# A linear-attention and feed-forward block on one core: later second x tile, block map on GpSimd, key and value products in two parts

## The chip, the core and the metric

The kernel runs on one core of a Trainium2 chip. Its engines run beside each other, each in its own program order: TensorE (PE, matrix products, with weight loads shown as PEld), VectorE (DVE), ScalarE (ACT), GpSimd (POOL) and SyncE (SP, which issues most of the transfers). They wait for each other through semaphores. The metric is the device time of one execution in microseconds (us).

## The reference

The input x has 2048 rows of 640 values, in bf16. The part that matters:

```python
def _A_ref(x, wqkv, w_phi, wo):          # H = 32 heads of Dh = 20
    q, k, v = split(x @ wqkv)
    pq = jnp.einsum("bhsd,hdf->bhsf", q, w_phi)
    pk = jnp.einsum("bhsd,hdf->bhsf", k, w_phi)
    phi_q = concat([softmax(pq), softmax(-pq)])
    phi_k = concat([softmax(pk), softmax(-pk)])
    kv  = jnp.einsum("bhsf,bhsd->bhfd", phi_k, v)
    z   = jnp.einsum("bhsf->bhf", phi_k)
    num = jnp.einsum("bhqf,bhfd->bhqd", phi_q, kv)
    den = jnp.einsum("bhqf,bhf->bhq", phi_q, z)[..., None] + 1e-6
    return (num / den).reshape(B, S, D) @ wo
def _B_ref(x, w1, w2):
    return silu(x @ w1) @ w2             # 640 -> 1728 -> 640
h  = x + _A_ref(layernorm(x), A_wqkv, A_w_phi, A_wo)
h2 = h + _B_ref(layernorm(h), B_w1, B_w2)
```

## The kernel before

The rows are cut into 16 tiles of 128 tokens (index t); the 640 features are five chunks of 128 (index c). The kernel is not written as loops over tiles. Each step is a small function `op_...`, and a long string `ORDER` lists the calls one by one, for all engines together: `kp.0@2` calls `op_kp(0)` with its PSUM result from bank 2 on, `xn.2.a` calls `op_xn(2, "a")`. The order of the calls is the order of the instructions on each engine; nothing reorders them. A letter at the end picks the engine: `v` DVE, `a` ACT, `p` POOL, `s` the SP queue for a transfer. PSUM has eight banks; a call that writes banks waits until what stood in them has been read.

The start, in words. `lx` loads tiles of x, `lk` chunks of the key weights, `lv` of the value weights, `lp` the small feature weights w_phi. `wm` is a product of constants into a bank that nobody reads; 14 of these stand at the head of PE's order and between its first steps. The feature weights are folded into the key weights: `wt` transposes a chunk of the key weights on PE, `wc` copies it out of PSUM (wTk), `mk` makes a mask with block-diagonal ones on POOL, `ph` multiplies w_phi with it into a block map `phb`, `fk` multiplies wTk with phb on PE, and `fc` casts the result into the folded weights Wfk, on ACT. `gk`, `gc` do the same for the query weights, whose transposed chunks come by a transposing transfer, `lq`.

For each tile: `st` takes the statistics (two halves and their sum, DVE), `rs` the reciprocal root with a power on POOL, `xn` the normalised tile; `xt` and `xc` transpose it through PE and PSUM, or `xd` by a transposing transfer on the SP queue. `kp` is the key projection with the folded weights, `vp` the value projection: ten products each, over five chunks and two halves of the output. `ke` takes the exponentials on ACT (plus and minus), `kr` their sums on DVE, `kn` divides (POOL, DVE or both by share: `p` all on POOL, `q` 48 of 64 groups, `b` 32, `d` 16, `v` none). `vc` copies the values out. `cc` sums keys times values into PSUM bank 7 over all tiles; `kc` and `km` turn the sum into the block matrix KVBD.

Then `qp`, `qs`, `qr`, `qt` are the query products in four parts (two, three, two and three products), `qe` their exponentials (EqT). `dp` multiplies EqT of one tile with KVBD into four PSUM banks, and `dw`, `dr`, `do` on DVE and POOL make num / den of it; `td` transposes that through SP. `op` multiplies with wo, `oa` adds to x, `sq`, `sr`, `hn`, `hd` are the second normalisation and transpose, `up`, `ua` the first feed-forward product and its silu, `yp`, `yh` the second, `yo`, `yz` add and store.

The order ends with the two parts of tile 13. Transfers are followed by eight semaphores in turn, so that the ninth transfer waits until the first has landed.

Of the kernel before, what the change touches and what calls it, by code (L numbers as in the profile page):

```python
# [30 lines left out]
lx.12.16.s vp.1@6 st.10 xt.2@5 vp.0@0 xc.2.a xn.9.a vc.0.a vp.2@2 st.11 lo.2.5.s xn.3.v xt.3@4 xc.3.a  # L31
rs.10.12 xn.8.a vc.2.a vc.1.a kp.2@0 ke.2 st.4 xd.9 st.5 kp.3@4 lo.0.2.s ke.3 rs.4.6 vp.3@2 xn.11.v vp.9@6
vc.9.a xn.4.a kp.9@0 ke.9 vc.3.a st.12 st.13 st.6 rs.12.14 xd.8 kr.1 kn.1.p kp.8@4 ke.8 mc.1 xn.13.a xn.12.a
xd.11 vp.11@6 vp.8@0 vc.8.a xn.5.v kr.0 kp.11@2 lq.2.s ke.11 st.7 rs.6.8 xn.6.a st.14 st.15 rs.14.16 xd.4
kr.9 vp.4@4 vc.4.a xd.5 vp.5@0 kn.0.p vc.11.a kr.2 vc.5.a kn.9.p kp.5@2 kr.11 kn.11.p gk.2@4 xn.10.a gc.2.a
xd.12 vp.12@6 vc.12.v kr.3 kn.3.p kp.4@0 xn.15.a ke.4 kp.12@4 cc.9 cc.1 kr.4 kn.4.p cc.0 xn.14.v cc.11 ke.5
kr.5 kn.2.d xd.13 ke.12 kr.12 lq.4.s xd.6 kp.6@0 lq.0.s ke.6 vp.13@2 vc.13.a kp.13@4 ke.13 vp.6@0 xd.15
xd.10 gk.4@2 vp.10@4 vc.6.a lq.3.s gk.3@0 gc.4.a gc.3.a vc.10.a kn.5.q kp.10@2 kn.12.p kr.6 xn.7.a l1.3.s
kn.6.q lq.1.s gk.1@0 gc.1.a kr.13 kn.13.p cc.4 cc.5 l1.0.s ke.10 kr.10 cc.2 cc.3 cc.12 xd.14 xd.7 kr.8
kn.8.p kn.10.d vp.15@4 vc.15.a kp.15@0 ke.15 kp.14@2 gk.0@4 gc.0.a vp.7@0 ke.14 kr.14 kn.14.p qp.0.1@4  # L40
# [10 lines left out]
dw.7.p dr.7 up.0.3@4 ua.0.3 do.6.0.p dp.8@0 dw.8.p dr.8 hn.2.a up.0.1@6 ua.0.1 td.6 do.8.0.p op.5@4 oa.5
dp.12@0 dw.12.p dr.12 yp.1.0@6 do.7.1.p do.7.0.p sq.5 td.7 hd.3 op.4@4 oa.4 sr.5 hn.5.v hd.5 do.9.1.p sq.4
td.9 sr.4 hn.4.a dp.10@0 dw.10.p yp.1.1 yp.0.1@4 yh.0.0 hd.2 hd.4 yo.1 dp.11@0 dw.11.p dr.11 do.8.1.p
do.11.0.p td.8 yp.0.0 yo.0 op.7@6 oa.7 sq.7 dr.10 op.6@0 oa.6 sq.6 sr.6 op.9@2 up.1.6@4 do.11.1.v td.11 oa.9
sq.9 dp.15@0 ua.1.6 sr.9 up.1.5@6 ua.1.5 up.1.1@4 hn.9.v hd.9 do.10.0.p dw.15.p dr.15 hn.6.v hd.6 op.8@6
oa.8 sq.8 op.11@0 ua.1.1 sr.7 hn.7.v hd.7 up.1.3@2 oa.11 do.12.1.p sr.8 hn.8.v do.15.0.p dp.14@4 dw.14.p
dr.14 do.14.0.v hd.8 ua.1.3 up.1.4@0 ua.1.4 do.14.1.v td.14 up.1.0@2 sq.11 sr.11 hn.11.v ua.1.0 up.2.6@4
ua.2.6 dp.13@0 dw.13.p dr.13 do.13.1.p up.2.0@6 up.2.5@4 ua.2.5 op.14@0 up.1.2@2 ua.2.0 oa.14 sq.14 up.2.2@4
ua.1.2 do.12.0.p td.12 sr.14 op.12@6 oa.12 ua.2.2 hn.14.v do.10.1.p do.15.1.v yp.4.0@0 up.2.4@2 ua.2.4 td.10
op.10@4 oa.10 up.2.1@6 sq.12 sr.12 hn.12.a hd.11 hd.12 up.2.3@2 ua.2.1 yp.2.0@4 ua.2.3 yp.9.0@6 do.13.0.p  # L60
# [4 lines left out]
up.4.3@0 ua.4.3 yp.14.0@2 yp.15.0@6 up.3.4@4 up.3.6@0 yh.4.0 yp.15.1 ua.3.4 ua.3.6 yp.11.0@4 yp.12.1@0 yo.15
yp.14.1 yo.14 yp.10.1@6 yh.3.1@2,3 yh.3.0 yp.10.0 yo.10 yp.12.0 yo.12 yp.11.1 yo.11 yp.13.0 yz.13.0.s
yp.13.1 yz.13.1.a
"""

@with_exitstack  # L70
def kernel(
# [194 lines left out]
    def op_wm(n=512):  # L266
        one = nc.const_aps.tensor
        nc.tensor.matmul(mm1()[:, 0:n], one(1.0, (P, P), BF16), one(1.0, (P, n), BF16), start=True, stop=True)  # L268

    def op_st(t):  # L270
        stats = sm.tile([P, 2, 6], F32, name="stats")
        for k in range(2):
            nc.vector.bn_stats(stats[:, k, :], X[:, t, k * 320 : (k + 1) * 320])  # L273
        nc.vector.bn_aggr(MV[:, t, :], stats[:])

    def op_rs(a, b):
# [86 lines left out]
            tl["gk", ce][:, 1, 0:320].rearrange("p (k r f) -> p k r f", k=2, r=C),  # L363
        )

    def proj(t, W):
        ps = mm2()
        for c in range(C):
            for half in range(2):
                nc.tensor.matmul(  # L370
                    ps[:, half, 0:320], tok(XnT[t // GT], t)[:, c, :], W[:, c, half * 320 : (half + 1) * 320],
                    start=(c == 0), stop=(c == C - 1),
                )
# [384 lines left out]
```

## Time and profile before

| what | value |
|---|---|
| median of 3 runs | 236.25 us (236.18 to 236.31) |
| the profiled execution | 236.35 us |
| its span | 234.4 us |
| TensorE busy | 230.5 us, 98% of the span |
| VectorE, ScalarE, GpSimd busy | 133.5, 114.5, 95.4 us |
| granted TensorE clock | 1.00 |

The span is the time from the first to the last instruction in the trace; about 2 us of the execution lie around it. In a row of the timeline stand the start, the time until the group ended, the engine, the line, the operation, what it writes and reads, and the count; in square brackets, how long the engine was idle before it and what ended that.

### The profile page before, as it was taken

To read this page: it belongs to the slowest core of one execution; us is meant where nothing else is said; L and a number is where in the kernel's file an instruction comes from. 1 tells how busy PE (TensorE), PEld (TensorE's weight loads), DVE (VectorE), ACT (ScalarE), POOL (GpSimd) and SP (SyncE) were. 2 spreads that over 40 slices of the span, in tenths; PEclk is the share of its full clock that TensorE was granted. 3 is DMA by queue.
4 is the path that set the end of the run, shared out by engine and by line. 5 is a ranking of instruction groups with operands and counts; after the bars stand their busy time and mean duration, and the time that the engine had idled before them with its cause. 6 is when DMAs were issued, how large, how long until landed. Compare 5 with 4: busy or idle time off the path is not lost.

```text
span 234.4 us, 6307 instructions
## 1 busy us (share of the span) xinstructions
PE 230.5 (98%) x2674; PEld 148.4 (63%) x2674; DVE 133.5 (57%) x249; ACT 114.5 (49%) x171; POOL 95.4 (41%) x190
## 2 busy tenths in 40 slices
PE   8999999999999999999999999999999999999995
PEld 4777777776554556876645455556776865566662
DVE  3999999999968899788956641301341310001132
ACT  3789996885857776742244536260040015613000
POOL 7485798997904455765285123141040000000000
PEclk9999999999999999999999999999999999999999
DMA  7967758839101375325823202123212300000112
GB/s 203 381 234 147 82 112 110 182 64 350 37 3 31 59 176 148 59 49 98 142 55 61 56 3 55 30 57 63 88 24 57 106 27 5 0 3 2 54 34 81
DMA packets 44844, 20.67 MB, mean 88 GB/s; under 512 B 34448, under 2 KB 44304, under 8 KB 44816
## 3 DMA queue, kind: packets, MB, share of 16 engines
q1 hardware_dynamic: 43728, 19.88, 36.1%
q10 hardware_dynamic: 1088, 0.39, 0.8%
q8 instruction: 21, 0.34, 0.6%
q14 instruction: 7, 0.06, 0.1%
HBM read 9.61 MB, written 2.62 MB: 52 GB/s over the span
## 4 chain that ended last, share of the span: by engine, by line
PE 98%; ACT 1%; DVE 0%; issue 0%
PE mm L691 24%; PE mm L645 24%; PE mm L370 19%; PE mm L457 10%; PE mm L566 9%; PE mm L504 3%; PE mm L268 2%; PE mm L427 2%; PE mm L337 1%; PE mm L655 1%; PE mm L704 1%; ACT EqT L479 1%; PE mm L322 1%; PE mm L308 0%; DVE ob L721 0%
## 5 line engine op out<-in xcount | busy, mean ns | idle before, releaser
L691 PE MATMUL mm<-w,shT 128*128 128x320 bf16 (+2 forms) x416 | 58.7, 299 | 0.0
L645 PE MATMUL mm<-HnT,w 128*128 128x512 bf16 (+1 forms) x325 | 58.6, 337 | 0.0
L691 PEld LDWEIGHTS <-shT 128*128 128x128 bf16 x416 | 39.6, 98 | 17.2 <-issue 1.1
L667 ACT ACTIVATE shT<-mm 128x1024 bf16<-128x1024 f32 (+2 forms) x29 | 27.6, 963 | 44.6 <-PE mm L645 43.1
L712 DVE TENSOR_TENSOR ob<-mm,X 128x640 bf16<-128x640 f32 x15 | 12.3, 819 | 62.3 <-PE mm L691 59.3
L645 PEld LDWEIGHTS <-w 128*128 128x128 bf16 x325 | 31.4, 98 | 23.2
L370 PEld LDWEIGHTS <-XnT 128*128 128x128 bf16 x320 | 30.8, 98 | 12.0
L414 POOL TENSOR_TENSOR Ek<-Ek,Sk 128x1280 bf16<-128x1280 bf16 (+2 forms) x15 | 32.9, 2217 | 4.0 <-DVE Sk L406 4.0
L539 POOL TENSOR_TENSOR o<-u,rd 128x320 bf16<-128x320 f32 x28 | 19.9, 727 | 22.9 <-DVE rd L533 16.4
L583 ACT ACTIVATE sq<-X 128x640 bf16<-128x640 bf16 x16 | 11.7, 732 | 28.3 <-DVE X L575 27.2
L566 PE MATMUL mm<-wo,ot 128*128 128x320 bf16 x160 | 23.9, 299 | 0.3 <-ACT EqT L479 0.3
L457 PE MATMUL mm<-XnT,Wfq 128*128 128x512 bf16 x100 | 23.8, 380 | 0.0
L370 PE MATMUL mm<-wv,XnT 128*128 128x320 bf16 x160 | 23.7, 299 | 0.0
L370 PE MATMUL mm<-Wfk,XnT 128*128 128x320 bf16 x160 | 23.5, 299 | 0.0
L395 ACT ACTIVATE Ek<-mm 128x640 bf16<-128x640 f32 x32 | 20.5, 714 | 6.0 <-PE mm L370 5.1
L403 DVE TENSOR_REDUCE Sk<-Ek 128x64 f32<-128x1280 bf16 x16 | 23.2, 1452 | 0.3 <-ACT Ek L395 0.3
L479 ACT ACTIVATE EqT<-mm 128x1024 bf16<-128x1024 f32 (+1 forms) x24 | 19.7, 879 | 4.9 <-PE mm L457 4.8
L575 DVE SCALAR_TENSOR_TENSOR X<-mm,X 128x640 bf16<-128x640 f32 x16 | 13.0, 818 | 15.4 <-PE mm L566 15.1
L566 PEld LDWEIGHTS <-ot 128*128 128x128 bf16 x160 | 15.7, 98 | 7.3 <-issue 0.2
L273 DVE BATCH_NORM_STATS2 stats<-X 128x6 f32<-128x320 bf16 x32 | 13.6, 467 | 3.8 <-DMA X<-in_A_x_dram 3.8
L457 PEld LDWEIGHTS <-Wfq 128*128 128x128 bf16 x100 | 9.1, 98 | 9.3
L525 DVE TENSOR_TENSOR u<-mm,w 128x672 f32<-128x672 f32 x16 | 13.7, 857 | 1.2 <-DVE w L523 0.3
(78 smaller groups left out, 204.3 us busy)
## 6 DMA issues: line engine op xcount, KB each, us to landing
out_dram<-ob SPq DMA_DIRECT2D x15, 160.0 KB, 1.8
...
```

Source lines behind the costliest of these rows:

```text
L370: nc.tensor.matmul(ps[:, half, 0:320], tok(XnT[t // GT], t)[:, c, :], W[:, c, half * 320 : (half + 1) * 320], start=(c == 0), stop=(c == C ...
L395: nc.scalar.activation(Ek[:, s, :].rearrange("p (a n) -> p a n", a=2), tl["kp", t][:, :, 0:320], AF.Exp, scale=1.0 - 2.0 * s,)
L403: nc.vector.tensor_reduce(Sk[:], tl["ek", t][:].rearrange("p s (h f) -> p (s h) f", f=DH), axis=AX.X, op=ALU.add,)
L414: nc.gpsimd.tensor_tensor(Ek3[:, 0:n], Ek3[:, 0:n], Sk[:, 0:n].unsqueeze(2).to_broadcast([P, n, DH]), op=ALU.mult,)
L457: nc.tensor.matmul(tl["qp", g, i][:, k, :], Wfq[:, c, r * P : (r + 1) * P], XnT[g][:, c, :], start=(c == 0), stop=(c == C - 1),)
L479: nc.scalar.activation(E[:, s, rs[0] : rs[-1] + 1, :], tl["qp", g, i][:, 0 : len(rs), :], AF.Exp, scale=1.0 - 2.0 * s,)
L525: nc.vector.tensor_tensor(u[:], A[1][:, :, :, 0:21], w[:].unsqueeze(3).to_broadcast([P, 4, 8, 21]), op=ALU.mult,)
L539: (nc.vector if eng == "v" else nc.gpsimd).tensor_tensor(tl["o", t][:, a * 320 : (a + 1) * 320].rearrange("p (h f) -> p h f", f=DH), tl["u ...
L566: nc.tensor.matmul(ps[:, half, 0:320], tl["ot", t][:, c, :], wo[:, c, half * 320 : (half + 1) * 320], start=(c == 0), stop=(c == C - 1),)
L645: nc.tensor.matmul(ps[:, i * W : (i + 1) * W], w1[:, c, fc * P : (fc + 1) * P], HnT[g][:, c, 0:W], start=(c == 0), stop=(c == C - 1), skip ...
L667: nc.scalar.activation(sh[:, a:b], tl["up", g, k][:, 0 : b - a], AF.Silu)
L691: nc.tensor.matmul(ps, shT[g][:, fc * W + i * P : fc * W + (i + 1) * P], w2[:, fc, a:b], start=first and fc == 0, stop=last and fc == FC - ...
```

## The change

The code changes in five places. The statistics are two steps, `sa` for the first half of a tile and `st` for the second half and the sum. `kp` and `vp` do the chunks 0 to 2, and new steps `kq` and `vq` do the chunks 3 and 4 into the same banks; the ten products are the same. `op_lt` takes a queue, but no call of it stands in the order. `ph` is called with `p` now. And `ORDER` is new from its first word to the last parts: the second x tile (`lx.1.2`) is loaded behind the four key chunks on SP, chunk 1 of the key weights is transposed ahead of chunk 0, there are 17 `wm` calls, and the order of tiles, the banks, and many engine letters differ further on.

```diff
-mk mo lx.0.1.a lk.0.1.s lp.a lx.1.2.s lk.4.5.a wm.512@7 wm.512@7 wm.512@7 wm.512@7 wm.512@7 wm.512@7
-wm.512@7 wm.512@7 wt.0@0 lk.1.2.s ta wc.0.a wm.256@2 wm.256@2 wm.256@2 wm.256@2 wm.256@2 wm.256@2 wt.1@1 wc.1.a st.0 rs.0.1
-ph.v fk.0@2 fc.0.a st.1 lk.2.3.s wt.2@4 wc.2.v lk.3.4.s wt.3@5 wc.3.v fk.1@6 fc.1.a rs.1.2 fk.2@0 fc.2.a
-lx.2.4.s xn.0.v lx.8.12.s wt.4@4 wc.4.v lv.0.3.s fk.3@2 fc.3.a xt.0@5 xn.1.v xc.0.v st.2 fk.4@6 fc.4.a
-rs.2.3 lv.3.5.s mc.0 xt.1@4 xc.1.a st.9 st.8 rs.8.10 lx.4.8.s st.3 rs.3.4 kp.0@0 ke.0 xn.2.a kp.1@2 ke.1
...
-mt qe.0.2 cc.15 cc.14 kc km.0 lh.s qp.3.0@4 qs.3.0 qr.3.0 km.1 dp.0@0 l1.4.s close dw.0.p dr.0 qt.3.0
-do.0.1.p qe.3.0 qp.2.0@6 qs.2.0 qr.2.0 qt.2.0 qe.2.0 do.0.0.p dp.1@0 dw.1.p qp.1.0@4 dr.1 do.1.0.p qs.1.0
...
-dp.4@0 dw.4.p td.2 sq.0 qp.2.2@5 qs.2.2 qe.2.2 op.1@6 oa.1 sr.0 qp.2.1@4 dp.6@0 dw.6.p l1.5.s l1.1.s qs.2.1
-qr.2.1 hn.0.a hd.0 sq.1 qt.2.1 sr.1 hn.1.v hd.1 qe.2.1 op.3@6 oa.3 sq.3 dp.5@0 dw.5.p op.2@4 sr.3 oa.2
...
+mo lx.0.1.a lk.0.1.s lp.a lk.1.2.s mk wm.512@7 wm.512@7 wm.512@7 wm.512@7 wm.512@7 wm.512@7 wm.512@7
+wm.512@7 wm.256@1 wm.256@1 wm.256@1 wm.256@1 wt.1@0 lk.4.5.a lk.2.3.s wt.0@1 wm.256@3
+wm.128@3 wt.2@2 lk.3.4.s sa.0 st.0 rs.0.1 ta wc.1.a lx.1.2.s xn.0.v xt.0@3 wt.3@4 xc.0.a wt.4@5 wc.3.a ph.p
+wm.256@0 wm.256@0 wm.128@0 fk.1@6 fc.1.a wc.0.v fk.0@0 fc.0.a wc.2.v fk.2@2 fc.2.a sa.1 st.1 rs.1.2 fk.3@6
+fc.3.a wc.4.v fk.4@4 lx.2.4.s sa.3 sa.2 xn.1.v kp.0@0 st.3 xt.1@2 xc.1.v rs.3.4 st.2 lv.0.3.s vp.0@6 kp.1@2
+fc.4.a kq.1 xn.3.v xt.3@4 kq.0 xc.3.a lx.8.12.s rs.2.3 sa.9 lv.3.5.s vq.0 kp.3@4 kq.3 sa.8 st.9 ke.1 lq.1.s
...
+mt cc.15 qp.2.0@2 kc km.1 qe.0.2 km.0 qp.3.0@0 qs.3.0 l2.6.8.s qr.3.0 close dp.0@4 dw.0.p dr.0 do.0.1.p
+qt.3.0 do.0.0.p qs.2.0 qe.3.0 qr.2.0 qt.2.0 qe.2.0 lo.0.2.s dp.1@4 dw.1.p dr.1 lh.s do.1.0.p qp.1.0@0 qs.1.0
...
+qp.3.2@0 dp.4@4 qs.3.2 qe.3.2 dw.4.p td.1 op.1@2 td.3 qp.2.1@0 dp.6@4 hn.0.a oa.1 sq.1 l2.0.2.s do.2.1.p
+td.2 sr.1 qs.2.1 qr.2.1 qt.2.1 qe.2.1 dw.6.p hd.0 qp.3.1@2 qs.3.1 hn.1.v dr.6 do.6.0.p dp.5@4 dw.5.p qr.3.1
+qt.3.1 qe.3.1 dr.4 do.4.0.p hd.1 do.4.1.p dr.5 do.5.1.p op.3@0 op.2@4 oa.3 sq.3 oa.2 dp.9@0 dw.9.p up.0.2@6
...
+    def op_sa(t):
+        tl["stats", t] = sm.tile([P, 2, 6], F32, name="stats")
+        nc.vector.bn_stats(tl["stats", t][:, 0, :], X[:, t, 0:320])
+
     def op_st(t):
-        stats = sm.tile([P, 2, 6], F32, name="stats")
-        for k in range(2):
-            nc.vector.bn_stats(stats[:, k, :], X[:, t, k * 320 : (k + 1) * 320])
+        stats = tl["stats", t]
+        nc.vector.bn_stats(stats[:, 1, :], X[:, t, 320:D])
         nc.vector.bn_aggr(MV[:, t, :], stats[:])
...
-    def proj(t, W):
-        ps = mm2()
-        for c in range(C):
+    def proj(t, W, ps, cs):
+        for c in cs:
...
     def op_vp(t):
-        tl["vp", t] = proj(t, wv)
+        tl["vp", t] = mm2()
+        proj(t, wv, tl["vp", t], range(3))
+
+    def op_vq(t):
+        proj(t, wv, tl["vp", t], range(3, C))
...
     def op_kp(t):
-        tl["kp", t] = proj(t, Wfk)
+        tl["kp", t] = mm2()
+        proj(t, Wfk, tl["kp", t], range(3))
+
+    def op_kq(t):
+        proj(t, Wfk, tl["kp", t], range(3, C))
```

More of the change, by code (lines that the diff above doesn't have):

```diff
@@ L31 @@
[L31 to L40, printed above, removed]
@@ L51 @@
[L51 to L60, printed above, removed]
@@ new lines @@
+fc.3.a wc.4.v fk.4@4 lx.2.4.s sa.3 sa.2 xn.1.v kp.0@0 st.3 xt.1@2 xc.1.v rs.3.4 st.2 lv.0.3.s vp.0@6 kp.1@2
+fc.4.a kq.1 xn.3.v xt.3@4 kq.0 xc.3.a lx.8.12.s rs.2.3 sa.9 lv.3.5.s vq.0 kp.3@4 kq.3 sa.8 st.9 ke.1 lq.1.s
+st.8 vc.0.a sa.10 st.10 xn.2.v ke.0 rs.8.10 ke.3 xn.9.v sa.11 lx.12.16.s xn.8.a vp.1@2 vq.1 xt.2@6 xc.2.v
+st.11 vp.3@0 vq.3 vc.3.a lx.4.8.s kp.2@6 sa.13 kq.2 sa.12 sa.4 sa.6 vc.1.a xd.9 xd.8 vp.2@4 vq.2 gk.1@0 ke.2
+rs.10.12 xn.11.a xd.11 gc.1.a vp.9@2 sa.5 vq.9 vc.9.a st.13 st.12 rs.12.14 kp.9@6 kq.9 st.4 xn.12.a lq.4.s
@@ new lines @@
+vc.2.a ke.9 kp.8@0 sa.7 kq.8 vp.8@2 vq.8 xn.10.v vp.11@4 xd.10 st.5 mc.0 rs.4.6 st.6 ke.8 vc.8.a st.7 rs.6.8
+xn.7.a kr.2 kn.2.p xd.12 kp.11@6 xn.4.a kq.11 ke.11 vq.11 vc.11.a xn.5.v kr.9 vp.10@0 kp.10@2 kq.10 ke.10
+kr.0 sa.14 xd.5 vp.12@6 sa.15 vq.12 gk.4@4 gc.4.a kn.9.p kr.3 xd.7 vp.5@2 xn.6.a vq.10 vc.10.a xn.13.a
+kp.5@4 kq.5 vp.7@0 lq.0.s vc.12.a vq.5 kn.0.p cc.9 cc.2 lq.2.s kn.3.p cc.3 st.15 st.14 rs.14.16 cc.0 xd.4
+vc.5.a xd.13 ke.5 vq.7 l2.10.13.s xn.14.a kp.12@2 kq.12 kr.11 kn.11.p vc.7.a kr.8 lq.3.s kn.8.p kp.4@4 xd.14
@@ new lines @@
+kq.4 kp.13@0 kq.13 ke.12 ke.4 gk.0@2 kr.10 l1.5.s ke.13 vp.13@4 vq.13 vc.13.a l1.1.s vp.4@0 vq.4 gc.0.a
+kp.14@4 kr.5 kn.5.q kq.14 cc.5 cc.8 xn.15.a cc.11 ke.14 kn.10.p cc.10 gk.2@2 qp.0.2@6 gc.2.a xd.6 vp.6@4
+kr.4 kn.4.p l2.4.6.s kr.12 vc.4.a vq.6 kr.1 vc.6.a kn.1.p kp.6@2 kq.6 kr.13 kn.13.p gk.3@0 gc.3.a kr.14
+kn.14.p xd.15 vp.14@4 vq.14 vc.14.v kp.7@0 kq.7 mc.1 ke.6 kr.6 ke.7 qp.0.1@2 qs.0.1 qr.0.1 kp.15@4 kq.15
+vp.15@0 l2.8.10.s ke.15 qt.0.1 cc.4 cc.1 kn.6.q l1.4.s l1.0.s qe.0.1 cc.6 l1.3.s kr.7 cc.13 kn.12.d kn.7.p
@@ new lines @@
+vq.15 vc.15.a qp.0.0@4 qs.0.0 l2.2.4.s qr.0.0 qt.0.0 qe.0.0 qs.0.2 cc.7 kr.15 kn.15.b cc.14 cc.12 lo.2.5.s
+mt cc.15 qp.2.0@2 kc km.1 qe.0.2 km.0 qp.3.0@0 qs.3.0 l2.6.8.s qr.3.0 close dp.0@4 dw.0.p dr.0 do.0.1.p
+qt.3.0 do.0.0.p qs.2.0 qe.3.0 qr.2.0 qt.2.0 qe.2.0 lo.0.2.s dp.1@4 dw.1.p dr.1 lh.s do.1.0.p qp.1.0@0 qs.1.0
+qr.1.0 td.0 qt.1.0 qe.1.0 qp.1.1@2 do.1.1.p dp.3@4 dw.3.p dr.3 qs.1.1 qr.1.1 qt.1.1 do.3.0.p qp.2.2@0 l1.2.s
+qp.1.2@1 dp.2@4 dw.2.p dr.2 do.2.0.p qe.1.1 qs.2.2 qe.2.2 qs.1.2 qe.1.2 do.3.1.p op.0@2 oa.0 sq.0 sr.0
@@ new lines @@
+qp.3.2@0 dp.4@4 qs.3.2 qe.3.2 dw.4.p td.1 op.1@2 td.3 qp.2.1@0 dp.6@4 hn.0.a oa.1 sq.1 l2.0.2.s do.2.1.p
+td.2 sr.1 qs.2.1 qr.2.1 qt.2.1 qe.2.1 dw.6.p hd.0 qp.3.1@2 qs.3.1 hn.1.v dr.6 do.6.0.p dp.5@4 dw.5.p qr.3.1
+qt.3.1 qe.3.1 dr.4 do.4.0.p hd.1 do.4.1.p dr.5 do.5.1.p op.3@0 op.2@4 oa.3 sq.3 oa.2 dp.9@0 dw.9.p up.0.2@6
+ua.0.2 up.0.3@4 ua.0.3 dp.7@0 dw.7.p do.6.1.p do.5.0.p td.4 up.0.0@6 ua.0.0 td.6 op.4@4 dr.9 do.9.0.p oa.4
+dr.7 sq.4 sr.3 sr.4 td.5 op.6@0 oa.6 dp.8@2 sq.6 dw.8.p hn.3.v up.0.1@6 op.5@0 do.9.1.p td.9 ua.0.1 hn.4.v
@@ new lines @@
+do.7.0.p do.7.1.v sq.2 td.7 dr.8 sr.2 hn.2.a hd.3 hd.2 hd.4 oa.5 dp.12@2 dw.12.p yp.1.1@6 yp.1.0 yh.0.0@0
+yo.1 dp.10@2 dw.10.p dr.10 do.10.1.v sq.5 do.8.0.p sr.5 hn.5.a do.8.1.p td.8 hd.5 yp.0.1 op.9@6 oa.9 sq.9
+sr.6 sr.9 yp.0.0 yo.0 op.7@2 oa.7 sq.7 sr.7 dp.14@4 dw.14.p op.8@0 oa.8 sq.8 sr.8 up.1.2@2 ua.1.2 up.1.1@4
+hn.7.v hn.9.v hd.9 hd.7 dr.12 do.10.0.p hn.6.v td.10 ua.1.1 up.1.0@6 dp.11@0 dw.11.p dr.11 up.1.4@4 hd.6
+do.11.1.v ua.1.0 hn.8.a ua.1.4 up.1.6@6 ua.1.6 dp.15@0 dw.15.p dr.15 do.15.0.v dr.14 up.1.5@4 ua.1.5 hd.8
@@ new lines @@
+up.2.6@6 ua.2.6 dp.13@0 op.10@4 do.11.0.v dw.13.p up.2.0@6 td.11 dr.13 do.13.0.v do.13.1.v td.13 ua.2.0
+do.15.1.v td.15 up.1.3@0 op.11@2 oa.11 do.14.0.p up.2.3@6 op.13@2 ua.1.3 yp.4.1@0 oa.13 ua.2.3 up.2.2@6
+ua.2.2 up.2.4@2 ua.2.4 oa.10 do.12.1.p do.12.0.v td.12 op.15@4 up.2.5@6 ua.2.5 do.14.1.p td.14 op.14@2 oa.14
+op.12@6 oa.12 sq.14 sr.14 hn.14.a yp.4.0 up.2.1@2 ua.2.1 sq.13 sr.13 hn.13.a yp.2.1@6 oa.15 yh.1.1@4,2 sq.10
+sr.10 hn.10.v yh.1.0 yp.2.0 yo.2 hd.10 yp.3.1 yo.4 sq.15 sr.15 sq.11 sr.11 hn.11.v sq.12 sr.12 yp.5.0
@@ new lines @@
+hn.15.v yp.3.0 yp.5.1 yo.5 yo.3 yp.9.1@6 yp.9.0 yh.2.0@0,2 hd.13 hd.11 yh.2.1@4 hn.12.a hd.12 yp.7.0 yp.7.1
+yo.7 yp.6.0 up.3.5@4 yp.8.0 ua.3.5 yo.9 up.3.0@6 up.3.3@4 ua.3.3 yp.6.1 yo.6 up.3.2@4 hd.15 yp.8.1 yo.8
+up.3.4@0 ua.3.4 up.3.1@2 ua.3.2 ua.3.0 up.3.6@0 ua.3.6 hd.14 up.4.2@4 up.4.1@6 ua.3.1 yp.10.1@0 yp.10.0
+ua.4.1 up.4.3@2 yh.3.0@6 yo.10 ua.4.2 up.4.0@4 ua.4.0 yp.11.0@0 yp.12.0 yp.12.1 yo.12 yp.11.1 yh.3.1@4,5
+yo.11 ua.4.3 yh.4.0@2,6 yp.14.1 yp.14.0 yo.14 yp.15.0 yp.15.1 yo.15 yp.13.0 yz.13.0.s yp.13.1 yz.13.1.a
@@ L253, in op_lt @@
     def op_lt(c, q="s"):
-        nc.sync.dma_start_transpose(wTk[:, :, c * P : (c + 1) * P], A_wqkv[c * P : (c + 1) * P, D : 2 * D])
+        (nc.sync if q == "s" else nc.scalar).dma_start_transpose(wTk[:, :, c * P : (c + 1) * P], A_wqkv[c * P : (c + 1) * P, D : 2 * D])
     def op_lo(a, b, q="s"):
```

14 lines of the change are left out of this document (removed).

## The prediction

> **What bounds the kernel now.** I read the page first (busy shares, then the chain that ended last), then the waits, then the timeline of the first 13 us and of the stage around 68 us, where both orders differ most.
>
> ```profile
> span 234.4 us, 6307 instructions
> PE 230.5 (98%) x2674; PEld 148.4 (63%) x2674; DVE 133.5 (57%) x249; ACT 114.5 (49%) x171; POOL 95.4 (41%) x190
> PE 98%; ACT 1%; DVE 0%; issue 0%
> PE mm L566 <- ACT EqT L479: 0.3, 1, 0.3
> ```
>
> TensorE (PE) is busy for 230.5 of 234.4 us and is 98% of the chain; among all waits, the one line of a PE matmul that waits in mid-stream is 0.3 us (line 566, products with wo). So the time is PE's list of products, plus what stands before its first useful stretch, plus its few gaps. The change alters no product's shape and no count except the warm-up ones on constants. It can therefore gain or lose only in the start and in gaps.
>
> ```profile
> 0.83 3.57 PE L268 MATMUL mm<-const-bfloat16-1.0 128*128 128x512 bf16 x8 [0.83 <-PEq L742]
> 4.73 1.49 PE L268 MATMUL mm<-const-bfloat16-1.0 128*128 128x256 bf16 x6
> 6.25 0.28 PEld L322 LDWEIGHTS <-wk 128*128 128x128 bf16 x5 [0.51 <-DMA wk<-in_A_wqkv_dram]
> 6.54 0.48 PE L337 MATMUL mm<-phb,wTk 128*128 128x140 bf16 x6
> 9.59 0.45 PE L308 MATMUL mm<-ident,xn 128*128 128x128 bf16 x5
> 9.99 2.89 PE L370 MATMUL mm<-Wfk,XnT 128*128 128x320 bf16 x20
> 12.72 1.52 PE L370 MATMUL mm<-wv,XnT 128*128 128x320 bf16 x10
> ```
>
> Until 6.2 us PE mostly runs products on constants, held by the second block of key weights; from 6.25 the folded key weights (line 337) and the transposes of x follow each other closely, and at 9.99 the projections begin and never stop. One projection product takes (12.72 - 9.99) / 20 = 0.136 us. My mark for comparing starts: both first x tiles transposed, six products of the first key projection done. Before, that is 9.99 + 6 x 0.136 = 10.81 us.
>
> **The change, part by part. The block map on GpSimd.** It is the input of every fold, so it decides when line 337's products begin.
>
> ```profile
> 5.99 0.88 DVE L273 BATCH_NORM_STATS2 stats<-X 128x6 f32<-128x320 bf16 x2
> 5.00 0.15 DVE L278 TENSOR_SCALAR RS<-MV 128x1 f32<-128x1 f32 x1
> 5.08 0.99 DVE L198 TENSOR_TENSOR phb<-phr,mask 128x800 bf16<-128x800 bf16 x1
> 5.24 1.24 POOL L281 TENSOR_TENSOR RS<-RS,nhalf 128x1 f32<-128x1 f32 x1 [0.75 <-DVE RS L278]
> 8.37 0.67 POOL L281 TENSOR_TENSOR RS<-RS,nhalf 128x1 f32<-128x1 f32 x1 [1.52 <-DVE RS L278]
> 9.10 0.44 DVE L297 TENSOR_SCALAR xn<-X,MV,RS 128x640 bf16<-128x640 bf16 x1
> 9.14 0.44 POOL L283 TENSOR_SCALAR RS<-MV,RS 128x1 f32<-128x1 f32 x1
> 11.24 0.55 POOL L281 TENSOR_TENSOR RS<-RS,nhalf 128x1 f32<-128x1 f32 x1 [1.66 <-DVE RS L278]
> L414 POOL TENSOR_TENSOR Ek<-Ek,Sk x15: 720/2356/3140, 24.2 to 61.6; 128x1280 bf16<-128x1280 bf16 x11, 128x320 bf16<-128x320 bf16 x2, 128x960 bf16<-128x960 bf16 x2
> 7.33 3.17 ACT L171 CAST Wfk<-mm 128x640 bf16<-128x640 f32 x5
> ```
>
> Before, the map took 0.99 us on VectorE (DVE) and was done at 6.07. In the new order GpSimd (POOL) makes it after the power and the scale of tile 0. The power beside the DVE map took 1.24, alone 0.55: with the map gone from DVE it runs 5.24 to 5.79. The first xn then runs on DVE at once, and the scale beside it takes 0.44 (row 9.14), a tenth after the power: to about 6.33. The map itself: POOL's two-input product with a broadcast took 0.72 for 320 elements at best and 2.356 for 1280, so 1.70 ns an element and 0.18 fixed, 1.54 for 800. It ends at 7.87; with the 0.06 that xn needed after its power (9.04 to 9.10), the first fold starts at 7.93 instead of 6.54. What hid the map before was the wait for the key weights until 6.25; that cover is passed.
>
> The price has bounds: 0.99 as on DVE (ends 0.55 earlier), and the slowest POOL row scaled, 3.140 x 800 / 1280 = 1.96 (ends 0.42 later). I take 1.54, the nearest form undisturbed. The Trainium skill, "GPSIMD Engine Reference", section "Engine selection", says that an elementwise operation on a tile belongs on VectorE, as GpSimd is about twice as slow with two inputs; the trace's ratio is 1.54 / 0.99. By the rule the map would take 2 x 0.99 = 1.98 and the sum below would end 0.44 later.
>
> **Key weights ahead of the second x tile, and the folds.** The second block now takes the second place of SP's queue, and each later one moves one place up; PE has warm-up products until about 5.05 (eight of 512, four of 256 columns, from rows 0.83 and 4.73), then the transposes of the weights and of x tile 0 and three more warm-ups, all over before 7.7. The place in the queue held the second x tile, whose statistics began at 5.99 without a wait, so the block is there by then; if only just then, six transposes of 0.29 and the warm-ups between end near 8.2, 0.2 later than the map allows. I take the earlier landing: this part is ready ahead of the map and gains nothing, and what is late next is the map. The second x tile is needed by its statistics only after 7 us. Then: the first fold runs 0.48 to 8.41, its cast on ScalarE (ACT) starts 0.04 later. Five casts took 3.17, the last 0.73, so 0.6 apart: they end at 9.15, 9.75, 10.35, 10.95, 11.55. The fourth fold reuses the first one's PSUM banks and waits for 9.15; two folds of 0.32 end at 9.87.
>
> **Key and value products in two parts.** The first part needs only three of the five casts: six products from 9.87 to 10.69 wait for none (third cast 10.35). The transpose of the second tile follows (0.29, as from 6.25 to 6.54), to 10.98. The next product uses the banks of the fourth cast, free at 10.95 and a semaphore: no wait worth counting. So the mark is passed at 10.98 against 10.81: **+0.15 us** rounded. Without the split, PE would have waited for the last casts, some 0.6 more. With the map at its two bounds the start is -0.4 to +0.6.
>
> **The orders behind.** Until the products with KVBD, DVE and POOL are nearly full:
>
> ```profile
> 24.00:50.00 26.00, 26.00 (x467) 19.48 (x465) 24.91 (x35) 23.10 (x40) 24.18 (x20) 1.00 0.68 107
> POOL Ek L414 <- DVE Sk L406: 4.0, 4, 1.4
> 66.26 1.68 PE L457 MATMUL mm<-XnT,Wfq 128*128 128x512 bf16 x7
> ```
>
> (busy PE, PEld, DVE, ACT, POOL). The new order shifts normalisations of Ek: tiles 2 and 10 wholly to POOL (+1.64 each), 7 to POOL (+2.36), 12 and 15 in part to DVE (-1.64, -1.1): POOL +2.9 us here, DVE less. POOL had 4.0 us of waiting for DVE's sums to give, and its last such product began at 61.6 while PE's last key-value products ended at 66.26. I take zero, with up to 1 us lost if POOL's pieces line up badly. The DMA transposes of xn are moved behind one transposed load of query weights and ahead of the loads of wo; SP is not PE's releaser in any row, so zero.
>
> Then comes the stage where products with KVBD hand four PSUM banks to DVE and take them again.
>
> ```profile
> 67.88 0.49 PE L504 MATMUL mm<-KVBD,EqT 32*128 32x44 bf16 x40
> 68.30 2.98 PE L457 MATMUL mm<-XnT,Wfq 128*128 128x512 bf16 x13
> 71.22 0.47 PE L504 MATMUL mm<-KVBD,EqT 32*128 32x44 bf16 x40
> 71.61 2.76 PE L457 MATMUL mm<-XnT,Wfq 128*128 128x512 bf16 x12
> 69.31 0.86 DVE L525 TENSOR_TENSOR u<-mm,w 128x672 f32<-128x672 f32 x1 [0.29 <-DVE w L523]
> 70.20 0.85 DVE L528 TENSOR_TENSOR u<-u,mm 128x672 f32<-128x672 f32 x1
> 73.28 0.85 DVE L528 TENSOR_TENSOR u<-u,mm 128x672 f32<-128x672 f32 x1
> 74.31 0.47 PE L504 MATMUL mm<-KVBD,EqT 32*128 32x44 bf16 x40
> 88.29 0.98 PE L566 MATMUL mm<-wo,ot 128*128 128x320 bf16 x6 [0.27 <-ACT EqT L479]
> ```
>
> Between tile 0 and tile 1 thirteen query products (2.92 us, start to start) cover DVE, which is done at 71.05, 2.75 after 68.30. In the new order one part (two products of 0.216) stands ahead of tile 0, so eleven are left: 2.49. DVE has 0.29 of first-use waits in that place and keeps them. PE waits 2.75 + 0.06 - 2.49 = **+0.32**. Two later handovers (after tiles 4 and 5) also have eleven products' worth of cover, 2.44; DVE there needs 71.61 to 74.13 as in the second round, about 2.5: **+0.1** for both, between 0 and 0.3. The wait of 0.27 at 88.29, for ACT's exponentials, goes: between the last of the query products whose exponentials free those banks and the wo products, the old order has ten wo products and a group on KVBD (1.36 + 0.6 = 2.0 us), the new one ten query products and a group (2.16 + 0.6 = 2.8): **-0.3**.
>
> **Sum.** +0.15 + 0.32 + 0.1 - 0.3 = +0.27 us. The profiled execution took 236.35 with a span of 234.4; the median of the three runs is 236.25, so the sum goes on the median: 236.5. About 0.2% (0.47 us) is what a measurement of this kernel can tell from no change, so this is no change with a lean to slower.
>
> **The rivals.** *The map comes later (slower).* Every tenth of POOL's map beyond 1.54 reaches PE one for one, since folds, casts and the first projection are chained behind it; at the slow bound (1.96) it is +0.42: 236.9. For it: line 414's longest is 3.140 against a median of 2.356. From 1.74 on, the sum is slower than before by over 0.2%. Against: on DVE only copies out of PSUM and statistics run meanwhile, and POOL's 0.55 at 11.24 ran beside statistics undisturbed.
>
> *POOL or DVE falls behind in the middle (slower).* If the normalisations reach PE's key-value products late, up to 1 us is lost: 237.3. For it: 24.91 of 26 busy on DVE. Against: 4.0 us of slack on POOL.
>
> *The start is won (faster).* If POOL makes the map at DVE's 0.99, the start gives -0.4; if DVE's first-use waits resolve sooner too, the two handovers cost nothing and only -0.3 remains: 236.25 - 0.7 = 235.6. For it: the cover in the first part is real, weights are ready early. Against: no POOL row with two inputs runs at DVE's pace.
>
> That the change does not do what it says: the built order has four key blocks ahead of x tile 1 on SP and the map on POOL, so no chance for that.
>
> **How the numbers follow.** Forecast 0.52 (its own range 236.2 to 236.9: 0.40 within 0.2%, 0.12 slower), late map 0.17, middle 0.08, won start 0.23. So faster 0.23, same 0.40, slower 0.37. The range 235.7 to 237.2 leaves out the far part of the won start and most of the middle rival, under 2 in 10.
>
> **What would show it.** Right: line 200's POOL row near 1.5 us ending near 7.9; first fold near 7.9; the value product of tile 0 near 11.0; a wait of about 0.3 ahead of the second group on KVBD; no wait of the wo products on ACT. Wrong: a map under 1.2 or over 1.9, or PE gaps between 20 and 66 us.

## The result, and the profile after

The changed kernel takes 237.2 us (median of 6 runs, 236.77 to 237.6), the kernel before, beside it, 236.29 (6 runs, 236.18 to 236.6): ratio 1.0036, 95% interval 1.0025 to 1.0047. It is slower by 0.9 us, which is more than 0.2%. The profiled execution took 236.77 (before: 236.35), the shortest of these six. Its page begins like the one before:

```profile
span 235.0 us, 6289 instructions
PE 228.0 (97%) x2657; PEld 147.9 (63%) x2677; DVE 131.6 (56%) x252; ACT 114.6 (49%) x171; POOL 95.3 (41%) x188
```

PE still sets the end, and its list of products is the same. (Its busy time is lower because 20 records of matmuls are missing from this trace: 2657 against 2677 weight loads.) The span is 0.6 longer, so the loss is in the start and in gaps. The start, from the timeline after; columns as before:

```profile
3.81 0.49 DVE L274 BATCH_NORM_STATS2 stats<-X 128x6 f32<-128x320 bf16 x1 [3.81 <-DMA X<-in_A_x_dram]
5.21 0.54 POOL L286 TENSOR_TENSOR RS<-RS,nhalf 128x1 f32<-128x1 f32 x1 [0.85 <-DVE RS L283]
5.79 0.45 DVE L302 TENSOR_SCALAR xn<-X,MV,RS 128x640 bf16<-128x640 bf16 x1 [0.66 <-POOL RS L286]
5.85 0.43 POOL L288 TENSOR_SCALAR RS<-MV,RS 128x1 f32<-128x1 f32 x1
6.24 1.52 POOL L200 TENSOR_TENSOR phb<-phr,mask 128x800 bf16<-128x800 bf16 x1
7.82 2.05 PE L342 MATMUL mm<-phb,wTk 128*128 128x140 bf16 x30 [0.23 <-POOL phb L200]
9.70 1.00 PE L374 MATMUL mm<-Wfk,XnT 128*128 128x320 bf16 x6
10.53 0.44 PE L313 MATMUL mm<-ident,xn 128*128 128x128 bf16 x5
10.86 0.84 PE L374 MATMUL mm<-wv,XnT 128*128 128x320 bf16 x5
```

One line leads from the landing of the first x tile (3.81) over statistics, power, normalisation and map (1.52, done at 7.76) to the folds, and six key products and five transposes later the mark is passed at 10.86, against 10.81 before. The later gaps, from PE's waits and from the timeline after:

```profile
PE mm L515 <- DVE u L539: 0.3, 1, 0.3
PE mm L438 <- issue: 0.2, 1, 0.2
```

```profile
48.26 1.09 PE L438 MATMUL mm<-Ek,Vp 128*21 128x40 bf16 x109
49.56 0.30 PE L438 MATMUL mm<-Ek,Vp 128*21 128x40 bf16 x19 [0.20 <-issue]
49.79 0.49 PE L342 MATMUL mm<-phb,wk 128*128 128x140 bf16 x6
60.72 1.20 PE L438 MATMUL mm<-Ek,Vp 128*21 128x40 bf16 x128
61.85 0.72 PE L374 MATMUL mm<-wv,XnT 128*128 128x320 bf16 x4
70.90 0.85 DVE L539 TENSOR_TENSOR u<-u,mm 128x672 f32<-128x672 f32 x1
71.81 0.46 PE L515 MATMUL mm<-KVBD,EqT 32*128 32x44 bf16 x40 [0.34 <-DVE u L539]
89.42 3.13 PE L577 MATMUL mm<-wo,ot 128*128 128x320 bf16 x20
90.12 0.85 DVE L539 TENSOR_TENSOR u<-u,mm 128x672 f32<-128x672 f32 x1
91.03 1.18 PEld L577 LDWEIGHTS <-ot 128*128 128x128 bf16 x9 [0.29 <-issue]
```

Three gaps are new. A key-value (KV) group of 128 products breaks off after 109 with no wait on it: from its start to what follows it takes 49.79 - 48.26 = 1.53, where the group at 60.72 takes 1.13, so 0.40 is lost. The second group on KVBD waits for DVE at 71.81 (0.39 from start to start, beyond the usual change of shape). And the wo products pause at 90.64 for 0.26 (start to start: from one product's start to the next one's, beyond the usual distance), until DVE has read the banks of the group on KVBD at 90.97. No wo product waits for ACT's exponentials any more: before, that pause was 0.34 start to start.

Profile against profile, in PE's starts: start +0.05; KV groups +0.26 (pauses of 0.38 and, in the last group, 0.11 now, of 0.13 and 0.10 before); second group on KVBD +0.39; wo products +0.26; the old wait -0.34. That makes +0.62, and PE's last product starts at 232.00 instead of 231.42, 0.58 later. The medians lie 0.9 apart, not 0.6, so something that this one execution does not show must vary between executions. The runs say the same: 236.77 to 237.6 now, 236.18 to 236.6 before.

### The profile page after: what moved, and what is told of

Read it like the earlier page. It is cut to its first block, busy times and chain, and to the rows that moved or that the text cites. A ratio compares the mean times of both kernels' runs of the same rounds, so it can differ in the third digit from the quotient of the medians.

```text
span 235.0 us, 6289 instructions
## 1 busy us (share of the span) xinstructions
PE 228.0 (97%) x2657; PEld 147.9 (63%) x2677; DVE 131.6 (56%) x252; ACT 114.6 (49%) x171; POOL 95.3 (41%) x188
## 4 chain that ended last, share of the span: by engine, by line
PE 92%; DVE 3%; DMA 1%; issue 1%; POOL 1%; ACT 0%; DVEq 0%
PE mm L656 24%; PE mm L702 24%; PE mm L374 19%; PE mm L577 9%; PE mm L468 8%; PE mm L515 3%; PE mm L438 2%; DMA X<-in_A_x_dram 1%; PE mm L342 1%; PE mm L666 1%; PE mm L715 1%; DVE u L536 1%; DVE u L539 1%; POOL phb L200 1%; DVE ob L732 0%
## 5 line engine op out<-in xcount | busy, mean ns | idle before, releaser
L425 POOL TENSOR_TENSOR Ek<-Ek,Sk 128x1280 bf16<-128x1280 bf16 (+3 forms) x16 | 35.3, 2239 | 0.0
L550 POOL TENSOR_TENSOR o<-u,rd 128x320 bf16<-128x320 f32 x23 | 16.4, 732 | 28.7 <-DVE rd L544 22.7
L374 PE MATMUL mm<-wv,XnT 128*128 128x320 bf16 x160 | 24.5, 299 | 0.0
L374 PE MATMUL mm<-Wfk,XnT 128*128 128x320 bf16 x160 | 24.0, 299 | 0.0
L468 PE MATMUL mm<-XnT,Wfq 128*128 128x512 bf16 x89 | 22.2, 379 | 1.2 <-issue 1.0
L539 DVE TENSOR_TENSOR u<-u,mm 128x672 f32<-128x672 f32 x16 | 13.7, 853 | 0.6
```

The source lines that it names most:

```text
L374: nc.tensor.matmul(ps[:, half, 0:320], tok(XnT[t // GT], t)[:, c, :], W[:, c, half * 320 : (half + 1) * 320], start=(c == 0), stop=(c == C ...
L425: nc.gpsimd.tensor_tensor(Ek3[:, 0:n], Ek3[:, 0:n], Sk[:, 0:n].unsqueeze(2).to_broadcast([P, n, DH]), op=ALU.mult,)
L468: nc.tensor.matmul(tl["qp", g, i][:, k, :], Wfq[:, c, r * P : (r + 1) * P], XnT[g][:, c, :], start=(c == 0), stop=(c == C - 1),)
L550: (nc.vector if eng == "v" else nc.gpsimd).tensor_tensor(tl["o", t][:, a * 320 : (a + 1) * 320].rearrange("p (h f) -> p h f", f=DH), tl["u ...
```

## The experiments

**1. The changed kernel once more.** No edit.

> The changed kernel itself, profiled a second time, to see which of its stalls are there in every execution. Between its profiled execution (236.77 us) and the median of its runs (237.2) lie 0.4 us. Theory: the waits on VectorE are fixed by the order (about 0.39 us ahead of the second group on KVBD, 0.26 ahead of the last wo products near 90.6), while the stall of 0.38 in the middle of a KV group near 49.2, in which no instruction carries a wait, changes its place and size; the median stays at 237.2 +- 0.2. Rival: the 0.38 comes back at the same product of the same group, so that it belongs to the order as well.

237.48 us (5 runs, 237.19 to 237.93), ratio 1.0049 [1.0037, 1.0061]. From its timeline:

```profile
4.09 0.49 DVE L271 BATCH_NORM_STATS2 stats<-X 128x6 f32<-128x320 bf16 x1 [4.09 <-DMA X<-in_A_x_dram]
6.54 1.52 POOL L197 TENSOR_TENSOR phb<-phr,mask 128x800 bf16<-128x800 bf16 x1
11.15 0.57 PE L371 MATMUL mm<-wv,XnT 128*128 128x320 bf16 x3
48.56 1.10 PE L435 MATMUL mm<-Ek,Vp 128*21 128x40 bf16 x109
49.85 0.30 PE L435 MATMUL mm<-Ek,Vp 128*21 128x40 bf16 x19 [0.19 <-issue]
62.41 4.17 POOL L422 TENSOR_TENSOR Ek<-Ek,Sk 128x1280 bf16<-128x1280 bf16 x2
65.59 1.41 PE L435 MATMUL mm<-Ek,Vp 128*21 128x40 bf16 x128
```

The rival holds: the stall in mid-group is back after the same 109 products. (Its size is not fixed, though: in two later traces with the same groups, the second run of experiment 3 and experiment 7, it is only 0.12.) Two things differ. The first x tile landed 0.28 later, and the map, the transposes and the mark (11.15) are later by 0.3. And the last KV group took 1.41 instead of 1.24, with a pause of 0.3 at its last tile, whose division ends on POOL at 62.41 + 4.17 = 66.58.

**2. The second x tile second in the queue again.**

```diff
-lp.a lk.1.2.s mk
+lp.a lx.1.2.s lk.1.2.s mk
...
-wc.1.a lx.1.2.s xn.0.v
+wc.1.a xn.0.v
```

> The new order with the second tile of x back in the second place of SyncE's queue, ahead of the second block of key weights. The prediction gave the earlier weights no worth, because the map on GpSimd would be late anyway (it ended at 7.76 in the profile after). By that the first fold stays at 7.8 and the time at 237.2. Rival: the second block lands near 6.2 instead of 4.3, and five groups of five transposes, three products on constants and the first x tile's transposes then end only near 8.3, so that the folds start 0.4 to 0.6 later: 237.6 to 237.8; then the load order is what makes room for the map on GpSimd.

237.54 us (6 runs), ratio 1.005 [1.0038, 1.0063], against 237.48 of experiment 1 on the same chip.

```profile
5.56 0.73 PE L323 MATMUL mm<-ident,wk 128*128 128x128 bf16 x10 [0.72 <-DMA wk<-in_A_wqkv_dram]
8.11 1.11 PE L338 MATMUL mm<-phb,wTk 128*128 128x140 bf16 x18 [0.23 <-POOL phb L196]
```

The first weight transposes wait until 5.56 (4.34 after), yet the first fold starts at 8.11, as in experiment 1, and it waits for the map. The new place of the second key block gains nothing, as predicted.

**3 and 4. New order in front with the old behind, and the reverse.** The cut is ahead of `kc`, behind the last KV group; the loads that one half issues and the other would repeat or miss were moved within the rest.

> The new order up to the last KV group, the old order from there on. Theory (both stages share the loss): the first part costs 0.05 us at the start and about 0.4 in the KV groups, the rest none: 236.7 to 236.8. Rival (the handovers of PSUM banks to VectorE are all of the loss): 236.3, no different from before. Rival (the first part is all of it): 237.2.

> The old order up to the last KV group, the new order from there on. Theory (both stages share the loss): 0.39 for the second group on KVBD and 0.26 at the wo products, less the 0.34 that the old order lost there: 236.6. Rival (handovers are all of it): 237.2. Rival (first part is all of it): 236.3.

Old in front, new behind: 236.4 us (11 runs), ratio 1.0004 [0.9995, 1.0013], no different from before. New in front, old behind: 238.13 (5 runs), ratio 1.0071 [1.0059, 1.0083], more than the whole change. The second has a wait of its own, from its timeline:

```profile
64.83 2.92 ACT L487 ACTIVATE EqT<-mm 128x1024 bf16<-128x1024 f32 x4 [1.41 <-PE mm L465]
67.61 0.46 ACT L449 CAST KVT<-mm 128x320 bf16<-128x320 f32 x1
69.04 0.56 PE L512 MATMUL mm<-KVBD,EqT 32*128 32x44 bf16 x40 [0.55 <-DVE KVBD L453]
```

The copy of KV stood behind exponentials on ACT, and PE waited for KVBD. So it was run again with the copy first:

```diff
-cc.15 qe.0.2 kc km.0 lh.s
+cc.15 kc qe.0.2 km.0 lh.s
```

> The earlier mixture (new order up to the last key-value group, old order behind it) with ScalarE's copy of KV ahead of its exponentials, so that PE does not wait 0.6 us for KVBD as it did there (238.13). Theory (the first part is all of the loss, the rest nets nothing, as the opposite mixture showed with 236.4): 237.2 to 237.5, as the new order. Rival (the rest loses 0.3 or more, and the opposite mixture hid it): 236.9 or less.

237.47 us (6 runs), ratio 1.0034 [1.0022, 1.0046]. By their medians the two mixtures now add up: the part in front loses about 1.0 us, the part behind nothing that shows (by the interval of the reverse mixture between -0.1 and +0.3; the terms there in the profile after, 0.39 + 0.26 - 0.34, are +0.31). The traces split the loss otherwise, as the account of the prediction shows. The reverse mixture has its mark at 10.62 although the first x tile landed only at 3.99: the old start does not follow that landing.

**5. The map earlier on POOL.**

```diff
+        if a == 0:
+            return
         if b - a == 1:
             nc.gpsimd.tensor_scalar(
                 out=RS[:, a, 1:2], ...
...
-ph.p wm.256@0 wm.256@0 wm.128@0 fk.1@6
+ph.p fk.1@6
```

> The new order without GpSimd's scale for tile 0 (0.43 us between the power and the map; its result is read only by a normalisation on ScalarE, and tile 0 is normalised on VectorE) and without the three products on constants ahead of the first fold. Theory (the map ends last, and folds, casts and first projection follow it one for one): the map starts 0.45 us earlier and the first key product with it, 9.25 in place of 9.70 where the first x tile lands at 3.8 (9.55 in place of 9.99 where it lands at 4.1); time 236.8. Rival (the casts on ScalarE or the second x tile's transposes hold the start): the folds move, the mark (six key products and the second x tile's transposes done) stays within 0.1 of 10.86, or 11.15 after the late landing; time 237.2 to 237.4. For the stall near 49.2 in mid-group the instruction stream is six instructions shorter here: if it comes at three products later in its group (111 in place of 108), it hangs on the place in the stream; if it stays at 108, on that group's own work.

238.33 us (5 runs), ratio 1.0085 [1.0071, 1.0099]: 0.85 slower than experiment 1. Neither theory. The start:

```profile
5.96 1.52 POOL L196 TENSOR_TENSOR phb<-phr,mask 128x800 bf16<-128x800 bf16 x1
6.03 1.63 DVE L300 TENSOR_SCALAR xn<-X,MV,RS 128x640 bf16<-128x640 bf16 x1 [0.66 <-POOL RS L282]
7.73 0.45 PE L311 MATMUL mm<-ident,xn 128*128 128x128 bf16 x5 [1.44 <-DVE xn L300]
```

The map came earlier (done 7.48), but DVE's normalisation, issued 0.07 behind it, took 1.63 instead of 0.45: it ended 0.18 after the map. It was blocked, and PE, which has the x transposes ahead of the folds, waited 1.44. The trace before has the same thing at 40.24: a normalisation issued into a GpSimd product that ended at 40.83 took 0.77 and ended 0.18 behind it. The short scale of tile 0 had been the cover under which the normalisation ran. The Trainium skill, "SBUF — State Buffer", section "Who interferes with whom", says that VectorE in its two-port modes and GpSimd share a pair of ports as a lock, and whoever issues second is blocked for the whole instruction. These rows agree that it is blocked; but it ended 0.18 after the product, less than the 0.45 that it takes alone, so by the profile's times the block ends a little before the product does. And the stall in mid-group:

```profile
49.32 1.13 PE L436 MATMUL mm<-Ek,Vp 128*21 128x40 bf16 x112
```

With six instructions fewer in the stream, the stall (0.31) comes after 112 products instead of 109, three products of two instructions later. Counted from the start of PE's list, it comes after 607 products here as in the profile after, and so in all nine traces that have it. It hangs on the place in PE's instruction stream, not on the tile.

**6. The KV groups.**

```diff
-kn.10.p cc.10 gk.2@2 qp.0.2@6
+kn.10.p gk.2@2 cc.10 qp.0.2@6
...
-kn.15.b
+kn.15.d
```

> The new order with two edits among the key-value groups: the fourth tile of the second group (tile 10) is moved behind the folds that follow it, and three quarters instead of half of the last normalisation (tile 15) go to VectorE, so that GpSimd is done earlier. Theory (the stall of 0.38 needs a long unbroken group of 8 ns products, and the stall of 0.1 to 0.3 ahead of the last tile of the last group is the wait for GpSimd): both go; time 236.7. Rival (the 0.38 hangs on a place in PE's instruction stream): it shows at about the same instruction, among the tiles moved there; only 0.1 to 0.3 is won: 237.0.

237.11 us (7 runs), ratio 1.003 [1.0019, 1.004].

```profile
48.63 0.98 PE L435 MATMUL mm<-Ek,Vp 128*21 128x40 bf16 x96
49.55 0.49 PE L339 MATMUL mm<-phb,wk 128*128 128x140 bf16 x6
49.97 0.38 PE L435 MATMUL mm<-Ek,Vp 128*21 128x40 bf16 x32
65.47 1.20 PE L435 MATMUL mm<-Ek,Vp 128*21 128x40 bf16 x128
117.75 0.99 PE L574 MATMUL mm<-wo,ot 128*128 128x320 bf16 x6 [0.37 <-DMA ot<-o]
```

Both pauses are gone from the KV groups: 0.92 + 0.30 = 1.22 for the 128 products around the folds, against 1.53. So the theory has the rows, but the time is near the rival's 237.0 and not 236.7. Nor is it the break in the group that removes the long pause: the first two kernels of experiment 8 have the same edit, and there PE pauses after 607 products again, for 0.27 and 0.57 (the last section says what differs). The median gained 0.1 to 0.4 against the changed kernel's two medians. This execution had the late x tile (mark at 11.23), and another wait that neither the prediction nor the first profile after has: the transposed attention tile for the wo products near 117 lands late. That pause was 0 in the profile after, about 0.1 in experiment 1, 0.56 in 2, 0.43 here, 0.60 in the first kernel of experiment 8.

**7. The key products of tile 0 in one piece.**

```diff
-fk.4@4 lx.2.4.s
+fk.4@4 fc.4.a lx.2.4.s
...
-kp.0@0 st.3 xt.1@2
+kp.0@0 kq.0 st.3 xt.1@2
```

(and `fc.4`, `kq.0` no longer at their old places)

> The new order with the key products of tile 0 in one piece again: its last four products stand behind the first six, ahead of the second x tile's transposes. Theory (the prediction's: without the split PE waits there for the last two of the five casts): PE's wait grows by 0.5 to 0.6 us near 10.5; time 237.7 to 237.8. Rival (the wait is paid later anyway, since the value weights or the second x tile's normalisation hold the next products): no change, 237.2 to 237.4.

238.35 us (4 runs), ratio 1.0081 [1.0067, 1.0095], 0.9 more than experiment 1.

```profile
9.95 1.00 PE L371 MATMUL mm<-Wfk,XnT 128*128 128x320 bf16 x6
11.11 0.43 PE L371 MATMUL mm<-Wfk,XnT 128*128 128x320 bf16 x2 [0.16 <-ACT Wfk L170]
11.71 0.43 PE L371 MATMUL mm<-Wfk,XnT 128*128 128x320 bf16 x2 [0.17 <-ACT Wfk L170]
15.67 0.31 PE L371 MATMUL mm<-Wfk,XnT 128*128 128x320 bf16 x1 [0.24 <-ACT XnT L170]
```

PE waits twice for ACT's casts, 0.33 each from start to start: 0.65, about the 0.6 that the prediction gave the split. Another 0.40 comes at 15.67, behind ACT's copy of the fourth tile, so the time is 0.5 above the 237.8 of the theory.

**8. Three other starts.** The block map first on POOL, with folds ahead of the first x tile and the edits of experiment 6; the same with the old order behind; and a third with the waits of these taken out one by one.

```diff
-lk.1.2.s mk wm.512@7
+lk.1.2.s mk ph.p wm.512@7
...
-lk.3.4.s sa.0 st.0 rs.0.1 ta wc.1.a lx.1.2.s xn.0.v xt.0@3 wt.3@4 xc.0.a wt.4@5 wc.3.a ph.p
+lk.3.4.s sa.0 st.0 rs.0.1 ta wc.1.a wc.0.v wc.2.v lx.1.2.s fk.1@6 fc.1.a wt.3@3 fk.0@0 fc.0.a xn.0.v
```

> The new order with another start: GpSimd makes the block map first, from 4.6 us, before the power of tile 0, while VectorE only waits and copies; folds of two column blocks stand ahead of the first x tile; both halves of the key and the value products of tile 0 follow before the second x tile. The two edits of the key-value groups (tile 10 behind the folds, three quarters of tile 15 on VectorE) are in too. Theory (the map's place on GpSimd, behind power and scale, is what makes the new start late): map done near 6.2, first fold at 6.2 to 6.6 in place of 7.8 to 8.1, the first x tile's normalisation not slowed (0.45, as beside no two-input work), first key product near 8.6; four more products done at 12.2 than before; 236.0 to 236.3. Rival (casts, VectorE's copies or the value weights hold the start): 236.9 to 237.1 as with the key-value edits alone.

> The same up to the last key-value group, and the old order behind it, with ScalarE's copy of KV ahead of its exponentials (in the earlier mixture of new and old order the exponentials stood first, and PE waited 0.6 us for KVBD). Theory (behind the key-value groups the new order wins and loses about equally: the old order followed by the new one was 236.4 against 236.38): the same time as the kernel with the new start alone, within 0.2. Rival (the waits of the new order for VectorE and for the transposed tile 8 near 117 cost more than what it saves): 0.3 to 0.5 faster than that.

> A third start: as in the kernel with the block map first on GpSimd, but with the last weight block's copy on ScalarE, the fourth tile of x loaded ahead of the value weights and the third behind them, value products and the second x tile's transposes ahead of the last four key products, and the second key group ahead of the value products' second part (where the earlier one waited 1.4 us for value weights). Key-value edits and the old order behind them are in, copy of KV first. Theory (the new order's loss is its start and its key-value groups, and the start can be made insensitive to the first x tile): first key product near 8.9, second x tile's transposes near 10.8, second tile's key products at 11.7, no wait over 0.3 before 16; 236.0 to 236.5, equal to or below before. Rival (whatever stands ahead, VectorE's chain for the second x tile, from statistics to the copy of its transposes, holds the next products): a wait of 0.5 or more ahead of the second tile's key products and 236.9 or more.

239.44 us (5 runs, 238.36 to 239.6), ratio 1.0117 [1.0098, 1.0135]; 238.85 (5 runs, 238.73 to 239.8), 1.0104 [1.009, 1.0118]; 237.29 (6 runs), 1.0035 [1.0023, 1.0047]. Rows of the first and, from 11.71 on, of the third:

```profile
4.87 1.52 POOL L196 TENSOR_TENSOR phb<-phr,mask 128x800 bf16<-128x800 bf16 x1 [0.51 <-DMA phr<-in_A_w_phi_dram]
6.93 0.45 DVE L298 TENSOR_SCALAR xn<-X,MV,RS 128x640 bf16<-128x640 bf16 x1
9.19 1.52 PE L370 MATMUL mm<-Wfk,XnT 128*128 128x320 bf16 x10
13.30 0.70 PE L370 MATMUL mm<-wv,XnT 128*128 128x320 bf16 x4 [1.26 <-DMA wv<-in_A_wqkv_dram]
51.60 0.65 PE L434 MATMUL mm<-Ek,Vp 128*21 128x40 bf16 x32
```

```profile
11.71 0.49 DVE L167 COPY XnT<-mm 128x640 bf16<-128x640 bf16 x1
12.26 1.53 PE L370 MATMUL mm<-Wfk,XnT 128*128 128x320 bf16 x10 [0.26 <-DVE XnT L167]
```

With the map first, the normalisation beside the short scale takes 0.45 again and the first key product comes at 9.19 instead of 9.70. But PE then waits for the value weights, which I had put a place too early. With that mended, it waits for the second tile's chain on DVE. Each time a start was won it was lost again within 5 us to what was late next. The times that the theories gave (236.0 to 236.3, the same within 0.2, 236.0 to 236.5) were all missed; the third kernel's is its rival's. The two kernels that differ only behind the KV groups have ranges that overlap, and I read nothing from their times. The row at 51.60 is the KV group's last tile, 0.65 against 0.38 in experiment 6, with the pause in it.

**9. The old start, with the KV edits and the new order behind.**

```diff
-xn.0.v xt.0@3 wt.3@4 xc.0.a wt.4@5 wc.3.a ph.p
+ph.v fk.0@2 fc.0.a sa.1 st.1 lk.2.3.s wt.2@4 wc.2.v lk.3.4.s wt.3@5 wc.3.v fk.1@6
```

> The old start (block map on VectorE, second x tile second, folds and transposes in the old order, key products of both tiles in one piece) up to the products of the first two tiles, then the new order with the two edits of the key-value groups. Theory (the new start loses 0.3 to 0.4 us in most executions, since it follows the landing of the first x tile one for one, which came 0.2 to 0.35 later than in the profile after in seven of nine profiles, while the old start at 3.99 in place of 3.83 was no later): mark at 10.6 to 10.8 and 0.3 to 0.5 less than with the key-value edits alone (237.11): 236.7. Rival (the start is not where the difference lies): 237.1.

237.4 us (6 runs), ratio 1.0035 [1.0023, 1.0047].

```profile
10.01 2.89 PE L370 MATMUL mm<-Wfk,XnT 128*128 128x320 bf16 x20
14.78 1.40 PE L370 MATMUL mm<-Wfk,XnT 128*128 128x320 bf16 x9 [0.24 <-ACT XnT L169]
```

The mark is at 10.84, 0.39 earlier than in experiment 6, as expected. But a wait of 0.40 (start to start) at 14.78, for ACT's copy of the fourth tile, gives it all back: the fortieth projection product starts at 16.01, in experiment 6 at 15.99. The time is neither the theory's 236.7 nor the rival's 237.1. How much of the median the start is worth stays open. No version beat the kernel before.

## Why the prediction was partly right

The forecast was no change with a lean to slower, 236.5; the time was 237.2, slower, at the upper end of the range. The forecast's own range ended at 236.9, and the rest of the stated range stood for rivals that did not come as told (the map itself took 1.52, not 1.96, and POOL's part in the middle is the smaller one), so that 237.2 still lies in it is in good part luck. Point by point:

- **The block map on POOL**: right. 1.52 us against 1.54, done at 7.76 against 7.87, first fold at 7.82 against 7.93. The bound at DVE's pace and the slow bound were both far off. The Trainium skill's rule ("GPSIMD Engine Reference", "Engine selection": twice as slow with two inputs) would have made it 1.98; here the ratio was 1.52 / 0.99 = 1.54.
- **Key weights ahead, split products**: right in this trace and by experiments 2 and 7 (0.65 for the split, where the text said 0.6).
- **The start, +0.15**: 0.05 in the profile, but 0.3 to 0.4 later in most other executions. The failed step is that the chain was dated by one landing of the first x tile. It landed at 3.81 and 3.85 in two and between 4.04 and 4.19 in nine of the eleven traces with the map on POOL. Why so often late was not tested: in the three traces with the old start it landed at 3.83, 3.85 and 3.99, and with the second x tile back in its place (experiment 2) at 4.10. The old start has cover there (3.99 and a mark of 10.62 in experiment 4); the new one has none, and the prediction said only that "that cover is passed", not that the landing now reaches PE.
- **"I take zero" for the middle**: wrong; this is the term that was missed, and PE gaps between 20 and 66 us were the prediction's own sign of being wrong. About 0.4 goes in mid-group at a fixed place of PE's instruction stream in both traces of the changed kernel, 0.1 to 0.3 at the last group. The second is a small case of the rival in which POOL falls behind: it works without a break until the last tile. The first is none of the rivals.
- **Second group on KVBD, +0.32**: 0.39. **Two later handovers, +0.1 (0 to 0.3)**: 0.26, all at the wo products. **The wait for exponentials, -0.3**: -0.34. All three mechanisms were as described; together (+0.31) they are at the edge of what the mixtures leave room for.
- The wait for the transposed tile near 117, 0 to 0.60, was in no step.

Together the terms of the profile explain its +0.6 of span. The usual execution is better read from experiment 1's trace, whose 237.48 is the median of its runs. Each row is set against the profile before; the last two stretches hold the same products in number and shape:

| stretch of PE's list | profile after | experiment 1 |
|---|---|---|
| up to the fortieth projection product | +0.04 | +0.33 |
| from there to the last KV product | +0.17 | +0.34 |
| from there to PE's last product | +0.37 | +0.61 |

That is 1.28 in experiment 1, where the medians lie 1.1 apart, so no large part is without a place. But the mixtures' medians put all of the loss in front, and the traces do not. With the new front ahead, the last stretch is 0.36 to 0.98 longer than before in the seven traces with the new order behind, and 0.25 to 0.28 in the three with the old order behind and the copy of KV first; behind the old front the new order costs 0.17, with only the old start (experiment 9) 0.48. So what the new order costs behind the KV groups seems to depend on what runs ahead of it. How the loss divides between front and rest stays open.
